# Attention and two feed-forward layers in one kernel: down products two gated blocks behind, and one rest subtracted from PSUM on VectorE

## The chip, the cores and the metric

One core of one Trainium2 chip runs the whole program. The time is the device time of one launch in microseconds; the median of three runs before the change is 899.72 us (898.28 to 900.67). Inputs and outputs are fp32.

## What is computed

The reference runs three parts in a row; the second and third take the one ahead as input. Sequence 576 and 4 batches make 2304 tokens.

```python
# attention: q, k, v of shape (4, 8, 576, 64), window of 128, a bias that falls with distance
scores = np.where(mask, scale * q @ k.T + bias, -1e9)
attn   = softmax(scores);  x = (attn @ v)            # tokens x 512
# first layer, d_ff 768
h = max(x @ w1, x @ w2, x @ w3);  y = h @ w_out      # tokens x 512
# second layer, d_ff 1536
g = y @ w_gate;  out = (g * sigmoid(g) * (y @ w_val)) @ w_out
```

## The kernel before

TensorE multiplies in the fast fp32r format, which keeps fewer bits. So every operand is held as two parts, a rounded head and the rest (operand minus head), and a product is three matmuls: head by head, head by rest, rest by head (`mm3`, L111 to L113, and L547 to L549 for the last product). `low` (L77) is the subtraction that makes a rest; `pool_round` (L80) rounds to a head on GpSimd. Weights come as 64-bit words and are turned into head and rest by `prep_w` (L90 to L99: two ScalarE and four VectorE instructions for a 128x512 tile).

The tokens are worked off in sub-chunks, (batch, half) with 256 and 320 tokens, for attention and the first layer. Attention goes in units of one head pair and one block of up to 128 queries: scores (L299, or L303 and L304), mask and softmax (L307 to L317), normalisation (L336 or L340), transposes (L349), mask selections on GpSimd (L365), values (L379 or L390), and the split of the result into head and rest. In the sub-chunks of batch 0 and the first of batch 1 the products are taken in plain fp32 (`native`), and the result comes out of PSUM in one piece: ScalarE writes the head into `x` (L384) and a copy `xr` (L385), and GpSimd subtracts the two (L77). The first sub-chunk (0, 0) has eight such units.

While the first sub-chunks are worked on, the 18 up weights of the first layer (names `w1_f_e`) are prepared; up products (`ps<-x,w`) of a sub-chunk run beside the attention of the next.

The second layer has chunks of 512 tokens (four, and a last one of 256) and 12 blocks of 128 hidden columns. `gate(c, f)` makes the two products of block f (`pg<-y,u`, 24 matmuls), then ScalarE's sigmoid (L532), two VectorE products (L533, L534), and on GpSimd the head (L80) and rest (L77) of the gated block `a`. `down(c, t, f)` multiplies block f with its output weight into PSUM (`po<-u,a`, 12 matmuls for a chunk of four tiles). The 36 weight tiles are named `u_n` with n = 3f + i: i = 0 gate, 1 value, 2 output weight. They are prepared during the end of the first layer and, three per block, in the first chunk's first blocks.

The written order sets the calls, and a list scheduler with its own timeline reorders the instructions of each engine by readiness and priority; each engine then runs its list strictly in that order. In the main loop the written order is, for block n: three weight preparations (first chunk), `gate` of block n + 1, `down` of block n. The next chunk's inputs are loaded at block `YAT`.

Of the kernel before, what the change touches and what calls it, by code (L numbers as in the profile page):

```python
# [23 lines left out]
NF1, NF2 = F1 // P, F2 // P  # L24
# [5 lines left out]
CHUNKS = [(t, min(TB, NT - t)) for t in range(0, NT, TB)]  # L30
# [3 lines left out]
C0, C1, C2, C3 = 5, 6, 12, 15  # L34
# [5 lines left out]
NORM0, K0 = "pp", 4  # L40
AH = 0, 100
A1, E1 = 3, 0
YAT = 8
LN, LT, LV = 1, 2, 4

LEAST = 1.0 * 2.0 ** -15
# [4 lines left out]
def kernel(ctx: ExitStack, tc, q0, k0, q1, k1, qk0, qk1, vv, w123, wo1, wgv, wo2, out):  # L51
# [10 lines left out]
    nc = tc.nc  # L62
# [13 lines left out]
    def low(eng, out, raw, head):  # L76
        eng.tensor_tensor(out=out, in0=raw, in1=head.bitcast(F32), op=ALU.subtract)  # L77
# [48 lines left out]
    def prep_up(f, e):  # L126
        if (f, e) not in w1:
            load_up(f, e)
        raw, w1[f, e] = w1[f, e], up_tile(f"w1_{f}_{e}")
        prep_w(raw, w1[f, e], pinned=PIN)  # L130
# [8 lines left out]
    def up_groups(b, s):  # L139

        n = SUBS[s][1]
        m = {}

        def group(f, e):
            xt = x_t[b, s]
            ps = ps_m.tile([P, 512], F32, tag="m", name="ps1")
            for k in range(KD):
                mm3(ps[:, :n], w1[f, e], k * P, xt[k][:, 0, :n], xt[k][:, 1, :n], k == 0, k == KD - 1)
            with tc.high_priority(HIGH):
                if e == 0:  # L150
                    m[f] = tmp.tile([P, 320], F32, tag="m0", name="m0")
                    nc.scalar.copy(m[f][:, :n], ps[:, :n])
                else:
                    nc.vector.tensor_tensor(out=m[f][:, :n], in0=ps[:, :n], in1=m[f][:, :n], op=ALU.max)
                if e == 2:
                    ht = hp.tile([P, 2, n], F32R, tag=f"h{s}", name=f"h{s}", bufs=NF1)
                    pool_round(ht[:, 0, :], m[f][:, :n])
                    low(nc.gpsimd, ht[:, 1, :], m[f][:, :n], ht[:, 0, :])
                    hs[b, s, f] = ht

        return [lambda f=f, e=e: group(f, e) for f in range(NF1) for e in range(3)]

    def down_groups(b, s):
        t0, n = SUBS[s]
        t0 += b * S

        def part(ps, d, ks):
            for k in ks:
                ht = hs[b, s, k]
                mm3(ps[:, :n], wo[k], d * P, ht[:, 0, :], ht[:, 1, :], k == 0, k == NF1 - 1)  # L170

        def group(ds):

            ps = [ps_m.tile([P, 512], F32, tag="m", name="ps2") for d in ds]
            for i, d in enumerate(ds):
                part(ps[i], d, range(NF1 - 1))
            for i, d in enumerate(ds):
                part(ps[i], d, [NF1 - 1])
                with tc.high_priority(HIGH):
                    y = tmp.tile([P, 2, 320], F32R, tag="y", name="y")  # L180
                    nc.scalar.copy(y[:, 0, :n], ps[i][:, :n])
                    low(nc.vector, y[:, 1, :n], ps[i][:, :n], y[:, 0, :n])
                nc.sync.dma_start(
                    out=y_dram[:, d * P:(d + 1) * P, t0:t0 + n].rearrange("a p n -> p a n"),
                    in_=y[:, :, :n].bitcast(F32),
                )

        return [lambda ds=ds: group(ds) for ds in ((0, 1), (2,), (3,))]
# [6 lines left out]
    prep = ea("prep", 4)  # L195
# [59 lines left out]
    def native(b, s):  # L255


        return b == 0 or (b, s) == (1, 0)
# [111 lines left out]
    def st_values(u):  # L370
        m = u.mq
        i0 = u.k0 // P
        v = pairs[u.b, u.s, u.p][2]
        pv = ps_v.tile([P, 2, 2, P], F32, tag="pv", name="pv")
        xr = small.tile([P, P], F32, tag="xr", name="xr")
        if native(u.b, u.s):
            for a in range(2):
                for i in range(i0, 2):
                    nc.tensor.matmul(  # L379
                        pv[a * D:a * D + D, 0, 0, :m], v[:, u.kb + i, a * D:a * D + D], u.t[:, i, 0, a, :m],  # L380
                        start=i == i0, stop=i == 1,
                    )
            xt = x_part(u)
            nc.scalar.copy(xt[:, 0], pv[:, 0, 0, :m])  # L384
            nc.scalar.copy(xr[:, :m], pv[:, 0, 0, :m])  # L385
            low(nc.gpsimd, xt[:, 1], xr[:, :m], xt[:, 0])
            return
        for a in range(2):
            for i in range(i0, 2):
                nc.tensor.matmul(  # L390
                    pv[:, a, :, :m], v[:, u.kb + i, a, :], u.t[:, i, :, a, :m], start=i == i0, stop=i == 1
                )
        c = small.tile([D, 2, P], F32, tag="c", name="c")
        nc.scalar.copy(c[:, :, :m], pv[D:P, :, 0, :m])
        nc.vector.tensor_tensor(out=c[:, :, :m], in0=pv[0:D, :, 1, :m], in1=c[:, :, :m], op=ALU.add)
        for a in range(2):
            nc.vector.tensor_tensor(
                out=xr[a * D:a * D + D, :m], in0=pv[0:D, a, 0, :m], in1=c[:, a, :m], op=ALU.add
            )
        split_x(u, xr)  # L400

    def x_part(u):
        m = u.mq
        n = SUBS[u.s][1]
        if (u.b, u.s) not in x_t:
            t = xp.tile([P, NP, 2, n], F32R, tag=f"x{u.s}", name=f"x{u.s}")
            x_t[u.b, u.s] = [t[:, p] for p in range(NP)]
        return x_t[u.b, u.s][u.p][:, :, u.q0:u.q0 + m]

    def split_x(u, xr):  # L410
        m = u.mq
        xt = x_part(u)
        pool_round(xt[:, 0], xr[:, :m])
        low(nc.gpsimd, xt[:, 1], xr[:, :m], xt[:, 0])
# [34 lines left out]
    for t in range(len(units) + LV):  # L449
        if t >= LV:  # L450
            u = units[t - LV]
            steps.append(lambda u=u: soon(st_values, u))
            if t + 1 == len(units) + LV or (units[t + 1 - LV].b, units[t + 1 - LV].s) != (u.b, u.s):
                done_at.append(len(steps))
        if 0 <= t - LT < len(units):
            steps.append(lambda u=units[t - LT]: soon(st_transpose, u))
        if 0 <= t - LN < len(units):
            steps.append(lambda u=units[t - LN]: soon(st_normalise, u))
        if t < len(units):
            u = units[t]  # L460
            if u.j == BLOCKS[u.s][0]:
                i = todo.index((u.b, u.s, u.p))
                if i == 0:
                    steps.append(begin)
                steps.append(lambda u=u, i=i: (soon(st_scores, u), prep_next(i + 1), load_next(i + 2)))
            else:
                steps.append(lambda u=u: soon(st_scores, u))
# [4 lines left out]
    def spread(main, *others, early=0):  # L472


        done = [0] * len(others)
        for i, g in enumerate(main):
            for n, o in enumerate(others):
                while done[n] < len(o) and done[n] * (len(main) - early) <= i * len(o):
                    o[done[n]]()
                    done[n] += 1  # L480
            g()
        for n, o in enumerate(others):
            for piece in o[done[n]:]:
                piece()
# [90 lines left out]
    conv = [lambda f=f, e=e: prep_up(f, e) for f in range(NF1) for e in range(3)]  # L575
# [16 lines left out]
    w2pool = en("w2pool")  # L592
    ps_o = en("ps_o", 4, space=PSUM)
    prep, load_y, gate, down = second(w2pool, raws2, ps_o)
    conv = [lambda f=f, i=i: prep(f, i) for f in range(NF2) for i in range(3)]
    spread(down_groups(*order[-2])[D6:] + up_groups(*order[-1]), [lambda: load_y(0, [0])] + conv[:C2])
    spread(down_groups(*order[-1]), [lambda: load_y(0, [1])] + conv[C2:C3])

    spread([lambda: gate(0, 0)], conv[C3:C3 + 3])
    blocks = [(c, f) for c in range(len(CHUNKS)) for f in range(NF2)]
    for n, (c, f) in enumerate(blocks):
        if c == 0:
            for piece in conv[C3 + 3 + 3 * f:C3 + 6 + 3 * f]:
                piece()
        if f == YAT and c + 1 < len(CHUNKS):
            load_y(c + 1)
        if n + 1 < len(blocks):
            gate(*blocks[n + 1])  # L610
        for t in range(CHUNKS[c][1] // P):
            down(c, t, f)

# [55 lines left out]
```

## Time and profile before

| | us |
|---|---|
| median of three runs | 899.72 |
| the profiled run's own time | 900.01 |
| its span, first to last instruction | 898.30 |
| TensorE busy | 878.1 (98%) |
| VectorE, ScalarE, GpSimd busy | 464.6, 349.5, 409.3 |
| mean granted TensorE clock | 0.996 of full |

The span is the time between the first and the last instruction of one profiled execution; the run's time has 1.7 us more around it. Busy times of TensorE are of modelled, overlapping matmuls, so start-to-start times tell more about a gap than busy time does. A wait is put down to whatever semaphore came last.

### The profile page before, as it was taken

How to read it: one execution, taken by the hardware profiler on the slowest of the kernel's cores; microseconds unless marked ns; L12 is line 12 of the kernel's file. 1: busy time of each engine (PE TensorE's matmuls, PEld its weight loads, DVE VectorE, ACT ScalarE, POOL GpSimd, SP SyncE). 2: the span in 40 equal slices, each digit the busy share in tenths (PEclk: the TensorE clock that was granted, in tenths of full speed). 3: DMA queues.
4: the chain of work that ended last, by engine and by line, in shares of the span. 5: the costliest groups of instructions: out<-in, count | busy, mean ns of one | idle time of the engine just before them, and what ended most of it. 6: DMA issues, size and time to landing. Idle time of an engine off the chain costs nothing.

```text
span 898.3 us, 14855 instructions
## 1 busy us (share of the span) xinstructions
PE 878.1 (98%) x5280; PEld 778.7 (87%) x5280; DVE 464.6 (52%) x1293; ACT 349.5 (39%) x1004; POOL 409.3 (46%) x599
## 2 busy tenths in 40 slices
PE   8998999999999999999998999999999999999998
PEld 6677899999999999999886788888888888888897
DVE  7689956867687776848999811111111111111111
ACT  6789656856486656614554301000110001000101
POOL 5587666766777586554325421222122212221222
PEclk9899999999999999999999999999999999999999
DMA  9844414415232431325755504000210002000100
GB/s 324 281 122 128 135 45 153 126 55 148 67 113 60 137 99 51 116 93 170 257 184 176 165 0 141 1 1 1 93 48 1 1 21 73 1 1 1 47 1 24
DMA packets 40873, 82.22 MB, mean 92 GB/s; under 512 B 3680, under 2 KB 16992, under 8 KB 40800
## 3 DMA queue, kind: packets, MB, share of 16 engines
q1 hardware_dynamic: 39712, 79.18, 27.5%
q10 hardware_dynamic: 1088, 2.10, 0.7%
q8 instruction: 42, 0.69, 0.3%
q14 instruction: 31, 0.25, 0.1%
HBM read 67.11 MB, written 14.16 MB: 90 GB/s over the span
## 4 chain that ended last, share of the span: by engine, by line
PE 81%; issue 6%; POOL 5%; DVE 4%; DMA 1%; ACT 1%; ACTq 0%; SPq 0%; POOLq 0%; DVEq 0%
PE ps L111 10%; PE pg L111 10%; PE pg L112 10%; PE pg L113 10%; PE ps L113 10%; PE ps L112 10%; PE po L549 5%; PE po L547 5%; PE po L548 5%; PE pv L390 2%; PE pt L349 2%; POOL a L80 1%; PE sc L299 1%; PE sc L304 1%; PE sc L303 1%
## 5 line engine op out<-in xcount | busy, mean ns | idle before, releaser
L80 POOL TENSOR_SCALAR a<-sg 128x512 fp32r<-128x512 f32 (+1 forms) x60 | 44.5, 742 | 331.8 <-DVE sg L534 328.5
L113 PE MATMUL pg<-y,u 128*128 128x512 f32 (+1 forms) x480 | 176.6, 368 | 0.0
L112 PE MATMUL pg<-y,u 128*128 128x512 f32 (+1 forms) x480 | 176.5, 368 | 0.0
L111 PE MATMUL pg<-y,u 128*128 128x512 f32 (+1 forms) x480 | 176.5, 368 | 0.0
L113 PE MATMUL ps<-x,w 128*128 128x256 f32 (+1 forms) x576 | 173.5, 302 | 1.6 <-DVE w L77 1.5
L111 PE MATMUL ps<-x,w 128*128 128x256 f32 (+1 forms) x576 | 173.3, 304 | 1.2 <-ACT w L99 1.2
L112 PE MATMUL ps<-x,w 128*128 128x256 f32 (+1 forms) x576 | 172.3, 300 | 1.9 <-POOL x L77 1.9
L533 DVE TENSOR_TENSOR sg<-pg,sg 128x512 f32<-128x512 f32 (+1 forms) x60 | 38.2, 637 | 253.8 <-ACT sg L532 253.8
L532 ACT ACTIVATE sg<-pg 128x512 f32<-128x512 f32 (+1 forms) x60 | 33.2, 553 | 325.2 <-PE pg L113 321.8
L113 PEld LDWEIGHTS ps<-x,w 128*128 128x128 f32 x576 | 109.2, 190 | 4.2 <-DVE w L77 2.4
L111 PEld LDWEIGHTS ps<-x,w 128*128 128x128 f32 x576 | 109.0, 190 | 4.0 <-ACT w L99 1.5
L112 PEld LDWEIGHTS ps<-x,w 128*128 128x128 f32 x576 | 109.2, 190 | 2.7 <-POOL x L77 2.1
L111 PEld LDWEIGHTS pg<-y,u 128*128 128x128 f32 x480 | 90.5, 188 | 15.5
L112 PEld LDWEIGHTS pg<-y,u 128*128 128x128 f32 x480 | 90.5, 188 | 15.3
L113 PEld LDWEIGHTS pg<-y,u 128*128 128x128 f32 x480 | 90.5, 188 | 15.1
L365 POOL TENSOR_SCALAR_AFFINE_SELECT t<-pk 128x512 fp32r<-128x512 f32 (+3 forms) x128 | 72.7, 590 | 34.7 <-PE pv L390 14.5
L549 PE MATMUL po<-u,a 128*128 128x512 f32 x216 | 84.2, 392 | 2.8 <-POOL a L77 2.8
L547 PE MATMUL po<-u,a 128*128 128x512 f32 x216 | 84.4, 391 | 0.3 <-POOL a L80 0.3
L548 PE MATMUL po<-u,a 128*128 128x512 f32 x216 | 84.2, 390 | 0.0
L77 POOL TENSOR_TENSOR a<-sg,a 128x512 fp32r<-128x512 f32 (+1 forms) x60 | 72.4, 1206 | 5.0
L317 ACT ACTIVATE z<-z,mn 128x128 f32<-128x128 f32 (+1 forms) x160 | 63.3, 399 | 21.8 <-DVE mn L312 21.8
L534 DVE TENSOR_TENSOR sg<-pg,sg 128x512 f32<-128x512 f32 (+1 forms) x60 | 38.2, 637 | 60.3 <-PE pg L113 60.1
(91 smaller groups left out, 1672.4 us busy)
## 6 DMA issues: line engine op xcount, KB each, us to landing
wr<-wgv SPq DMA_DIRECT2D x24, 512.0 KB, 4.2
qkr<-qk SPq DMA_DIRECT2D x24, 416.0 KB, 3.4
wr<-w SPq DMA_DIRECT2D x18, 512.0 KB, 5.2
wr<-wo SPq DMA_DIRECT2D x12, 512.0 KB, 3.9
y<-y_dram SPq DMA_DIRECT2D x12, 512.0 KB, 4.1
y_dram<-y SPq DMA_DIRECT2D x16, 320.0 KB, 2.4
out<-ob SPq DMA_DIRECT2D x18, 256.0 KB, 2.1
y_dram<-y SPq DMA_DIRECT2D x16, 256.0 KB, 2.9
```

The lines of the kernel that those rows point to most:

```text
L77: eng.tensor_tensor(out=out, in0=raw, in1=head.bitcast(F32), op=ALU.subtract)
L80: nc.gpsimd.tensor_scalar(out=out, in0=in_, scalar1=1.0, scalar2=1.0, op0=ALU.mult, op1=ALU.mult)
L111: nc.tensor.matmul(ps, wh, xt_h, start=first, stop=False)
L112: nc.tensor.matmul(ps, wh, xt_l, start=False, stop=False)
L113: nc.tensor.matmul(ps, wl, xt_h, start=False, stop=last)
L317: nc.scalar.activation(out=z[:m, a], in_=z[:m, a], func=AF.Exp, scale=-1.0, bias=mn[:m, a:a + 1], accum_out=sm[:m, a:a + 1],)
L365: nc.gpsimd.affine_select(out=t[:, i, :n, :, :m], in_=w[:, :n, :, :m], compare_op=op, fill=0.0, base=0, pattern=[[0, n], [0, 2], [-sign, m ...
L533: nc.vector.tensor_tensor(out=sg, in0=pair[0], in1=sg, op=ALU.mult)
L534: nc.vector.tensor_tensor(out=sg, in0=pair[1], in1=sg, op=ALU.mult)
L547: nc.tensor.matmul(po, ah, w2[f, 2][:, 0, :], start=f == 0, stop=False)
L548: nc.tensor.matmul(po, ah, w2[f, 2][:, 1, :], start=False, stop=False)
L549: nc.tensor.matmul(po, al, w2[f, 2][:, 0, :], start=False, stop=f == NF2 - 1)
```

## The change

There are two parts. In the second layer, `gate` of blocks 0 and 1 is issued ahead of the loop and the loop issues `gate` of block n + 2 ahead of `down` of block n; the weight preparations are put in the order of that need, and the next chunk's inputs are loaded at block 6 instead of 8. In attention, for the eight units of sub-chunk (0, 0) alone, the rest is formed by VectorE straight from PSUM, without `xr` and without GpSimd.

```diff
-YAT = 8
+YAT = 6
@@ st_values
             nc.scalar.copy(xt[:, 0], pv[:, 0, 0, :m])
+            if (u.b, u.s) == (0, 0):
+                low(nc.vector, xt[:, 1], pv[:, 0, 0, :m], xt[:, 0])
+                return
             nc.scalar.copy(xr[:, :m], pv[:, 0, 0, :m])
             low(nc.gpsimd, xt[:, 1], xr[:, :m], xt[:, 0])
@@ second layer
-    conv = [lambda f=f, i=i: prep(f, i) for f in range(NF2) for i in range(3)]
+    blocks = [(c, f) for c in range(len(CHUNKS)) for f in range(NF2)]
+    need = [(f, i) for f in range(2) for i in range(2)]
+    for f in range(NF2):
+        need += [(f + 2, i) for i in range(2) if f + 2 < NF2] + [(f, 2)]
+    conv = [lambda f=f, i=i: prep(f, i) for f, i in need]
...
-    spread([lambda: gate(0, 0)], conv[C3:C3 + 3])
+    spread([lambda: gate(0, 0), lambda: gate(0, 1)], conv[C3:C3 + 3])
...
-        if n + 1 < len(blocks):
-            gate(*blocks[n + 1])
+        if n + 2 < len(blocks):
+            gate(*blocks[n + 2])
```

On TensorE, at the down products of block 1 (output weight `u_5`) in the second layer, before; `u_7` is the value weight of block 2:

```order
L111 MATMUL pg_7156<-y_6844,u_7_6671 128x512
L112 MATMUL pg_7156<-y_6844,u_7_6671 128x512
L113 MATMUL pg_7156<-y_6844,u_7_6671 128x512
L547 MATMUL po_7097<-u_5_6605,a0_7093 128x512
L548 MATMUL po_7097<-u_5_6605,a0_7093 128x512
L549 MATMUL po_7097<-u_5_6605,a1_7094 128x512
```

The same place after the change, where `u_10` is the value weight of block 3 and lines 550 to 552 are the old 547 to 549:

```order
L111 MATMUL pg_7182<-y_6836,u_10_6704 128x512
L112 MATMUL pg_7182<-y_6836,u_10_6704 128x512
L113 MATMUL pg_7182<-y_6836,u_10_6704 128x512
L550 MATMUL po_7123<-u_5_6743,a0_7045 128x512
L551 MATMUL po_7123<-u_5_6743,a0_7045 128x512
L552 MATMUL po_7123<-u_5_6743,a1_7046 128x512
```

The gate products of block 3 now stand ahead of the down products of block 1.

On GpSimd, in the first sub-chunk (normalisations `z`, mask selections `t`, rests `x0`), before:

```order
L365 AFFINE_SELECT t_296<-pk_295 128x256 x2
L77 TENSOR_TENSOR x0_328<-xr_325,x0_328 128x128
L336 TENSOR_SCALAR z_346<-z_346,rc_371 128x128 x2
L325 TENSOR_SCALAR sm_389<-sm_389 128x2
L77 TENSOR_TENSOR x0_328<-xr_354,x0_328 128x128
L336 TENSOR_SCALAR z_387<-z_387,rc_407 128x128 x2
L365 AFFINE_SELECT t_366<-pk_365 128x256 x2
```

The same stretch of GpSimd after:

```order
L365 AFFINE_SELECT t_296<-pk_295 128x256 x2
L336 TENSOR_SCALAR z_345<-z_345,rc_369 128x128 x2
L325 TENSOR_SCALAR sm_387<-sm_387 128x2
L336 TENSOR_SCALAR z_385<-z_385,rc_404 128x128 x2
L365 AFFINE_SELECT t_364<-pk_363 128x256 x2
```

The two rests are gone from between the normalisations. On VectorE they stand among the weight preparation; the place of the first one, after:

```order
L94 SCALAR_TENSOR_TENSOR wf_237<-wr_200,wf_237 128x512
L307 COPY_PREDICATED sc_408<-later_111,fill_112 128x2x128
L331 RECIPROCAL rc_369<-sm_347 128x2
L77 TENSOR_TENSOR x0_328<-pv_324,x0_328 128x128
L96 SCALAR_TENSOR_TENSOR wr_200<-wr_200,wf_237 128x512
L93 TENSOR_SCALAR wf_306<-wf_306 128x512
```

The fourth row is new; the other five stood there before in this order.

## Rows read from the trace of the kernel before

**Rows 1.** The profile page: busy time, share of the span and instructions by engine.

```profile
PE 878.1 (98%) x5280; PEld 778.7 (87%) x5280; DVE 464.6 (52%) x1293; ACT 349.5 (39%) x1004; POOL 409.3 (46%) x599
```

**Rows 2.** Waits of TensorE: who waited for whom, us in total, times, longest.

```profile
PE po L549 <- POOL a L77: 2.8, 4, 0.9
...
PE ps L112 <- POOL x L77: 1.9, 1, 1.9
...
PE po L547 <- POOL a L80: 0.3, 1, 0.3
```

**Rows 3.** Timeline of TensorE, second layer: start, us, instruction [idle before <-releaser].

```profile
465.13 0.39 PE L547 MATMUL po<-u,a 128*128 128x512 f32 x1
...
483.54 0.39 PE L548 MATMUL po<-u,a 128*128 128x512 f32 x1
484.57 0.50 PE L549 MATMUL po<-u,a 128*128 128x512 f32 x1 [0.65 <-POOL a L77]
...
519.17 0.39 PE L547 MATMUL po<-u,a 128*128 128x512 f32 x1
...
527.33 0.39 PE L547 MATMUL po<-u,a 128*128 128x512 f32 x1
```

**Rows 4.** Stages: start:end length, busy us (count) by engine, PEclk, DMA share, GB/s.

```profile
490.00:500.00 10.00, 9.38 (x42) 7.41 (x41) 9.97 (x16) 4.20 (x8) 5.00 (x3) 1.00 0.55 175
```

**Rows 5.** Timeline of VectorE, second layer: products of two gated blocks.

```profile
485.93 0.68 DVE L533 TENSOR_TENSOR sg<-pg,sg 128x512 f32<-128x512 f32 x1
...
488.67 0.68 DVE L534 TENSOR_TENSOR sg<-pg,sg 128x512 f32<-128x512 f32 x1
...
495.05 0.68 DVE L533 TENSOR_TENSOR sg<-pg,sg 128x512 f32<-128x512 f32 x1
```

**Rows 6.** Timeline of GpSimd, second layer: with and without weight preparation on VectorE.

```profile
489.43 2.53 POOL L80 TENSOR_SCALAR a<-sg 128x512 fp32r<-128x512 f32 x1 [4.91 <-DVE sg L534]
492.05 1.59 POOL L77 TENSOR_TENSOR a<-sg,a 128x512 fp32r<-128x512 f32 x1
...
528.31 0.62 POOL L80 TENSOR_SCALAR a<-sg 128x512 fp32r<-128x512 f32 x1 [6.17 <-DVE sg L534]
529.01 1.28 POOL L77 TENSOR_TENSOR a<-sg,a 128x512 fp32r<-128x512 f32 x1
```

**Rows 7.** Stages of the first 100 us; columns PE, PEld, DVE, ACT, POOL, PEclk, DMA.

```profile
10.00:15.00 5.00, 4.36 (x29) 3.18 (x27) 4.47 (x23) 4.53 (x19) 4.15 (x12) 1.00 1.02 403
15.00:20.00 5.00, 4.07 (x28) 2.87 (x27) 4.92 (x18) 4.67 (x19) 4.84 (x8) 1.00 1.05 391
20.00:25.00 5.00, 3.72 (x25) 2.40 (x25) 4.65 (x18) 4.18 (x14) 4.75 (x10) 1.00 1.04 394
25.00:30.00 5.00, 3.76 (x18) 2.66 (x18) 3.66 (x12) 0.86 (x5) 2.79 (x6) 0.76 1.05 384
30.00:35.00 5.00, 5.00 (x22) 3.94 (x21) 1.33 (x7) 3.84 (x15) 2.41 (x5) 0.55 1.02 367
95.00:100.00 5.00, 5.00 (x38) 5.00 (x38) 5.00 (x13) 3.92 (x15) 1.96 (x3) 1.00 0.51 171
```

**Rows 8.** Timeline of VectorE, first 100 us: two idle times and the last weight rest.

```profile
31.93 0.29 DVE L312 CUSTOM_DVE_ANT_0 z<-sc,bias 128x128 f32<-128x128 f32 x1 [2.12 <-PE pt L349]
...
34.92 0.43 DVE L307 COPY_PREDICATED sc<-later,sc 128x256 f32<-128x256 int16 x1 [1.74 <-PE sc L299]
...
94.98 0.96 DVE L77 TENSOR_TENSOR w<-wr,w 128x512 fp32r<-128x512 f32 x1
```

**Rows 9.** Timeline of GpSimd: two rests of the first sub-chunk.

```profile
14.80 0.88 POOL L77 TENSOR_TENSOR x<-xr,x 128x128 fp32r<-128x128 f32 x1
...
24.54 1.64 POOL L77 TENSOR_TENSOR x<-xr,x 128x128 fp32r<-128x128 f32 x1
```

**Rows 10.** One line's instructions: ns min/median/max, first and last start us, forms.

```profile
L397 DVE TENSOR_TENSOR xr<-pv,c x104: 206/283/286, 146.2 to 404.9; 64x128 f32<-64x128 f32 x80, 64x64 f32<-64x64 f32 x24
L385 ACT COPY xr<-pv x28: 210/270/290, 13.4 to 140.2; 128x128 f32<-128x128 f32 x24, 128x64 f32<-128x64 f32 x4
```

More of the change, by code (lines that the diff above doesn't have):

```diff
@@ L594 @@
     prep, load_y, gate, down = second(w2pool, raws2, ps_o)
-    conv = [lambda f=f, i=i: prep(f, i) for f in range(NF2) for i in range(3)]
+    blocks = [(c, f) for c in range(len(CHUNKS)) for f in range(NF2)]
[3 more added lines that the diff above has]
+    conv = [lambda f=f, i=i: prep(f, i) for f, i in need]
     spread(down_groups(*order[-2])[D6:] + up_groups(*order[-1]), [lambda: load_y(0, [0])] + conv[:C2])
     spread(down_groups(*order[-1]), [lambda: load_y(0, [1])] + conv[C2:C3])
-    spread([lambda: gate(0, 0)], conv[C3:C3 + 3])
-    blocks = [(c, f) for c in range(len(CHUNKS)) for f in range(NF2)]
+    spread([lambda: gate(0, 0), lambda: gate(0, 1)], conv[C3:C3 + 3])
     for n, (c, f) in enumerate(blocks):
```

## Prediction

> **What bounds the kernel now.** The share of busy time comes first: TensorE 98%, every other engine about half [rows 1]. So the time is TensorE's work plus what TensorE loses, and the change removes none of its products: 5,280 stay 5,280. The question is only where it loses time. The list of TensorE's waits names the two places that the change touches: the down products (L547, L549) wait for GpSimd's halves of the gated block, and an up product (L112) waits 1.9 us for GpSimd's rest of the attention result [rows 2]. Both lists are short because a modelled matmul end hides part of each gap, so I measure the loss by start times instead.
>
> In the second layer, the down products of blocks 1, 7 and 8 start at 465.13, 519.17 and 527.33 us [rows 3]. Without preparation beside them, blocks lie 8.16 us apart (7 to 8). From 1 to 7 six blocks took 54.04 us, where 6 x 8.16 = 48.96: TensorE loses 5.1 us there. Inside such a block the third product, L549, starts 1.03 us after the one ahead of it and is put down to GpSimd [rows 3]. The pace is VectorE's: it is busy 9.97 of 10 us [rows 4], and its first product of a gated block comes at 485.93 and again at 495.05, 9.12 us later [rows 5]. With that VectorE load GpSimd's rounding takes 2.53 us and its subtraction 1.59; once VectorE is free, 0.62 and 1.28 [rows 6]. The gated block is late for two reasons, VectorE's queue and GpSimd's long instructions, and the down products follow only one block behind.
>
> In the first 100 us the load is on the other engines. From 10 to 25 us VectorE, ScalarE and GpSimd are each over 80% busy and TensorE waits between them; from 25 to 35 us there is a hole: VectorE does 3.66 + 1.33 us of work in 10, and the granted clock falls to 0.76 and 0.55 in those stretches [rows 7]. From 95 us TensorE is full [rows 7], one block after the last rest of an up weight is made at 94.98 [rows 8]. So what delays VectorE's weight preparation before 95 us delays everything behind it, and what TensorE saves there stays saved.
>
> **Part one: down products two blocks behind.** It adds no instruction. Each gated block gets 8.16 us more (one gate product group and one down group) before it is wanted. VectorE does 9.12 us of work for a block where TensorE needs 8.16 [rows 3, 5], so TensorE gains 0.96 us on it per block, over the six blocks in which weights are prepared at most 5.8 us. The added 8.16 us cover that with 2.4 us to spare, and the stall does not come back as another: the PSUM buffers of a gate group are needed again two groups later in both orders, and the two scratch tiles of the gate are freed by GpSimd's subtraction, which then ends some 5 us after VectorE's second product [rows 5, 6]. So I take the whole 5.1 us. The lower bound is what the list of waits shows, 2.8 + 0.3 = 3.1 us [rows 2]. The new preparation order (gate and value weights of two blocks first, the output weight of a block when its down products are near) is the same 36 weights on the same VectorE; it is hidden by the distance of the preparation, whose last rest is needed only in the last blocks. Without that cover a missing weight would cost 2.5 to 3 us, a third of the 9.12. The later chunks' inputs are loaded at block 6 instead of 8, since their gate now comes a block earlier; nothing is queued behind those loads on SP's queue but output stores of a chunk's end. Cost nothing; a late load would show as a TensorE wait at a chunk's start. The end of the kernel keeps its last three product groups: nothing.
>
> **Part two: the first sub-chunk's rest on VectorE.** Removed: eight copies on ScalarE of 0.27 us [rows 10] and eight GpSimd subtractions. The two in the rows took 0.88 and 1.64 us [rows 9], and TensorE's 1.9 us wait ends with the second. The order also shows GpSimd's mask selections move up behind the normalisations. Added: eight VectorE subtractions of 128x128 from PSUM. No row shows that form; the nearest is L397 (PSUM and SBUF into SBUF, 128 columns), 0.283 us [rows 10], so 8 x 0.28 = 2.2 us. Below nothing it cannot be. VectorE is 89 to 98% busy from 10 to 25 us [rows 7], so the five or so that fall there cost their full time, 1.4 us; those in the hole are hidden. Each also waits for ScalarE's head, and behind it in VectorE's queue stand the weight preparation and the next scores.
>
> The gain has two ends. At least the 1.9 us wait of TensorE goes [rows 2]. At most the whole hole of VectorE goes: 10 - 3.66 - 1.33 = 5.0 us [rows 7], since its two long idle times, 2.12 and 1.74 us, end with TensorE's transposes and scores [rows 8], which stood behind the blocked product. I take the middle, 3.4 us, since the removed wait is directly ahead of the hole but not its only cause. Net: -3.4 + 1.4 = -2.0 us, with ends of -1.9 + 2.2 = +0.3 and -5.0 + 1.4 = -3.6.
>
> The rest of the schedule moves too: four attention units fewer stand ahead of the last up weight on VectorE. That is 8 softmax inputs, 3 mask copies and 3 key rests, some 5 us by L312's and L307's rows at 0.29 and 0.43 us [rows 8] and about 0.6 us for a key rest (an estimate). But TensorE loses about as much work of its own to later, so I count nothing, with an end of -2.7. Against it, the last attention result of the second sub-chunk is ready later; a late one costs at most a GpSimd subtraction, 1.6 us [rows 9].
>
> A GpSimd subtraction of one size takes 0.88 or 1.64 us here, and the rounding 2.53 or 0.62 [rows 6, 9]: beside a busy VectorE it stretches. The Trainium skill (SBUF — State Buffer, Who interferes with whom) says that a VectorE instruction with at most one SBUF input, outside the two-port modes, does not contend with GpSimd; the new subtraction reads one operand from PSUM, so by that rule it adds nothing to GpSimd's time. If it stretched GpSimd as the rows show for other work, part two's gain would shrink by up to 0.8 us each. No row of this form can show which.
>
> **Sum.** The profiled run took 900.01 us (span 898.30, 1.71 around it), 0.29 above the median of 899.72. 900.0 - 5.1 - 2.0 = 892.9, against the median 892.6.
>
> **The rivals.**
> - The hole closes and the clock stays up. For it: GpSimd has no spare time ahead of the hole. Against: VectorE and ScalarE are nearly as full, so TensorE stays as idle as it was. The Trainium skill (TensorE: Matmul & The Clock Gate, Part 1) says that the throttled state is the default and activity releases it; the two low clock rows behind the thinly used stretch agree. Price: -3.6 and the clock of 30 to 35 us, 5 x 0.45 = 2.25 us [rows 7]. 900.0 - 5.1 - 3.6 - 2.2 = 889.1, or 888.8.
> - Part two brings nothing, because VectorE's pace to 95 us swallows it: 900.0 - 5.1 = 894.9, or 894.6.
> - Part two costs: VectorE waits at two of the rests for about 2 us each [rows 8]: 898.9, or 898.6.
> - Part one does not do what it says: the late VectorE products keep TensorE at 9.12 us per block through scratch or PSUM buffers: 900.0 - 2.0 = 898.0, or 897.7.
> - Slower: VectorE's queue blocks at the rests. Five of the eight stand where the attention chain is slow; each waits 1.93 us, the mean of 2.12 and 1.74 [rows 8], with the weight preparation behind it: 9.7 + 2.2 = 11.9 us, 906.5. It decides from 7.8 us on (5.1 and the 2.7 us of the bound below). Against it: VectorE has 5 us of idle time there already.
>
> **How the numbers follow.** About 0.3%, 2.7 us, is what a measurement of this kernel can tell from no change: faster means under 897.0, slower over 902.4. Forecast 892.6 with its own range of 890 to 894.5: 0.45. Hole and clock: 0.17. Part two nothing: 0.17. Part two costs: 0.07. Part one without effect: 0.07. Slower: 0.07. Faster 0.79, same 0.14, slower 0.07. The range leaves out the slower case and half of each end: 888 to 898.
>
> **What would show it.** Part one: down products 8.1 to 8.2 us apart from the second block on, no wait of L547 or L549 for GpSimd, and GpSimd's 2.5 us roundings still there. Part two: L112's wait for the result gone, VectorE's idle times in 25 to 35 us shorter, the last up weight ready 1 to 4 us before 94.98. The prediction is wrong if the second layer shows new waits on the gate's own products, if VectorE sits idle ahead of the PSUM subtractions, or if the middle of the kernel, which I left out (100 to 435 us), moves by more than 1 us.

## The result, and the profile after

The changed kernel takes 891.6 us (median of four runs, 888.6 to 892.0) where the kernel before took 899.5 beside it: a ratio of 0.9906, 95% interval 0.9884 to 0.9927. Measured again in another group it was 891.1 and 0.9906 (0.9878 to 0.9935). The forecast was 892.6. The profiled execution took 892.0 us with a span of 890.30.

The page's busy times, and the first rows of TensorE's waits (who waited for whom, us in total, times, longest), to be held against [rows 1, 2]:

```profile
PE 875.6 (98%) x5280; PEld 777.8 (87%) x5280; DVE 467.8 (53%) x1301; ACT 347.8 (39%) x996; POOL 401.1 (45%) x591
```

```profile
PE sc L299 <- DVE mn L312: 2.2, 5, 0.6
PE pt L349 <- ACT z L340: 1.3, 1, 1.3
...
PE pg L111 <- DVE y L77: 0.8, 1, 0.8
```

The down products are gone from the list, and so is the up product that waited 1.9 us for the attention result. VectorE has eight instructions more, ScalarE and GpSimd eight less each. The two longest of the new waits are shown: transposes wait for ScalarE's `z`, and a gate product for `y`.

Timeline of TensorE in the second layer, lines 550 to 552 being the old 547 to 549 [rows 3]: the layer's first gate product and the gap behind it, the starts of blocks 1, 5, 7 and 8, and the one gap left between blocks.

```profile
441.61 0.39 PE L111 MATMUL pg<-y,u 128*128 128x512 f32 x1
...
446.85 0.39 PE L113 MATMUL pg<-y,u 128*128 128x512 f32 x1
448.05 0.50 PE L111 MATMUL pg<-y,u 128*128 128x512 f32 x1 [0.81 <-DVE y L77]
...
467.22 0.39 PE L550 MATMUL po<-u,a 128*128 128x512 f32 x1
...
499.86 0.39 PE L550 MATMUL po<-u,a 128*128 128x512 f32 x1
500.09 0.39 PE L551 MATMUL po<-u,a 128*128 128x512 f32 x1
500.62 0.50 PE L552 MATMUL po<-u,a 128*128 128x512 f32 x1
...
516.63 0.39 PE L550 MATMUL po<-u,a 128*128 128x512 f32 x1
...
524.79 0.39 PE L550 MATMUL po<-u,a 128*128 128x512 f32 x1
```

Blocks 1 to 7 now take 49.41 us instead of 54.04; each lies 8.16 behind the one ahead but block 6, at 8.61. VectorE is as full as before in 490 to 500 us (9.97 of 10 [rows 4]), but TensorE notices it only ahead of block 6.

The first 100 us, where [rows 7] had the hole from 25 to 35 us (columns PE, PEld, DVE, ACT, POOL, PEclk, DMA share, GB/s):

```profile
25.00:30.00 5.00, 4.14 (x26) 2.96 (x25) 4.42 (x15) 4.38 (x15) 2.56 (x4) 1.00 1.05 383
30.00:35.00 5.00, 4.92 (x33) 3.02 (x32) 4.62 (x21) 4.28 (x15) 2.32 (x4) 1.00 1.06 378
70.00:75.00 5.00, 3.07 (x12) 1.75 (x13) 3.75 (x16) 4.16 (x16) 2.05 (x6) 0.70 0.00 0
75.00:80.00 5.00, 5.00 (x34) 4.88 (x32) 4.37 (x12) 0.85 (x6) 3.29 (x7) 0.62 0.27 82
```

VectorE's idle time in 25 to 35 us fell from 5.0 to 1.0 us and the granted clock is full there. But another hole opens at 70 us, and the granted clock is at its lower level (1.2 of 2.4 GHz) from 72.0 to 78.8, about as long as before from 27.6 to 34.5. These rows show how it opens (GpSimd, VectorE, ScalarE, TensorE):

```profile
65.42 3.34 POOL L365 TENSOR_SCALAR_AFFINE_SELECT t<-pk 128x128 f32<-128x128 f32 x2
...
70.93 0.22 DVE L331 RECIPROCAL rc<-sm 64x2 f32<-64x2 f32 x2 [2.25 <-POOL sm L325]
...
71.13 1.28 ACT L340 ACTIVATE z<-z,rc 64x128 f32<-64x128 f32 x4 [0.84 <-DVE rc L331]
...
71.58 0.58 PE L349 MATMUL pt<-ident,z 64*128 64x64 f32 x2 [1.31 <-ACT z L340]
```

Two GpSimd mask selections take 3.34 us together beside a nearly full VectorE (3.29 us of work in the 3.40 from 65.4 us on). The tiny sum behind them in GpSimd's queue, with four other instructions between (L325, adding 1e-9 to the softmax's denominator), comes late, VectorE's reciprocal waits 2.25 us for it at the head of its queue, and TensorE's transposes 1.31 us behind that.

**Where the time went**, by the start of the same product in the two profiled executions. From block 1 on the changed kernel has one gate group (24 of the 36 products of a block, 5.44 us) more behind it, which is taken off here. Each of the two executions holds one stretch at the lower clock of some 7 us in the first 100 us. The first gate product before:

```profile
446.06 0.39 PE L111 MATMUL pg<-y,u 128*128 128x512 f32 x1
```

| | before | after | difference |
|---|---|---|---|
| first gate product of the second layer | 446.06 | 441.61 | -4.45 |
| down products of block 1 | 465.13 | 461.78 | -3.35 |
| down products of block 7 | 519.17 | 511.19 | -7.98 |
| span | 898.30 | 890.30 | -8.00 |

So attention and first layer gave 4.45 us, the start of the second layer took 1.1 back (0.97 of it in the gap at 446.85), its blocks gave 4.63, and the rest is equal: from block 7 to the end both take 379.1 us. The earlier load of the next chunk's inputs, which was not run alone, changes nothing there that can be seen.

### The profile page after: what moved, and what is told of

It reads as the page before. It is cut to its first block, busy times and chain, and to the rows that moved or that the text cites. A ratio compares the mean times of both kernels' runs of the same rounds, so it can differ in the third digit from the quotient of the medians.

```text
span 890.3 us, 14848 instructions
## 1 busy us (share of the span) xinstructions
PE 875.6 (98%) x5280; PEld 777.8 (87%) x5280; DVE 467.8 (53%) x1301; ACT 347.8 (39%) x996; POOL 401.1 (45%) x591
## 4 chain that ended last, share of the span: by engine, by line
PE 83%; issue 6%; POOL 4%; DVE 3%; DMA 1%; ACT 1%; ACTq 0%; SPq 0%; POOLq 0%; DVEq 0%
PE ps L113 10%; PE ps L111 10%; PE ps L112 10%; PE pg L113 9%; PE pg L111 9%; PE pg L112 9%; PE po L552 5%; PE po L550 5%; PE po L551 5%; PE pv L393 2%; PE sc L299 2%; PE pt L349 2%; POOL a L80 1%; PE pv L379 1%; PE sc L304 1%
## 5 line engine op out<-in xcount | busy, mean ns | idle before, releaser
L112 PE MATMUL pg<-y,u 128*128 128x512 f32 (+1 forms) x480 | 176.6, 368 | 0.0
L111 PE MATMUL ps<-x,w 128*128 128x320 f32 (+1 forms) x576 | 172.4, 303 | 1.1 <-ACT m L152 0.8
L113 PE MATMUL ps<-x,w 128*128 128x320 f32 (+1 forms) x576 | 173.2, 302 | 0.1
L112 PE MATMUL ps<-x,w 128*128 128x320 f32 (+1 forms) x576 | 172.6, 300 | 0.0
L112 PEld LDWEIGHTS ps<-x,w 128*128 128x128 f32 x576 | 109.5, 190 | 1.2 <-issue 0.9
L112 PEld LDWEIGHTS pg<-y,u 128*128 128x128 f32 x480 | 90.5, 188 | 15.5
L365 POOL TENSOR_SCALAR_AFFINE_SELECT t<-pk 128x512 fp32r<-128x512 f32 (+3 forms) x128 | 81.0, 655 | 46.2 <-PE pv L393 20.5
```

The source lines that it names most:

```text
L111: nc.tensor.matmul(ps, wh, xt_h, start=first, stop=False)
L112: nc.tensor.matmul(ps, wh, xt_l, start=False, stop=False)
L113: nc.tensor.matmul(ps, wl, xt_h, start=False, stop=last)
L365: nc.gpsimd.affine_select(out=t[:, i, :n, :, :m], in_=w[:, :n, :, :m], compare_op=op, fill=0.0, base=0, pattern=[[0, n], [0, 2], [-sign, m ...
```

## The experiments

Ratios are against runs of the kernel before on the same chip, with 95% intervals.

**Each part alone.** First part two alone:

```diff
             nc.scalar.copy(xt[:, 0], pv[:, 0, 0, :m])
+            if (u.b, u.s) == (0, 0):
+                low(nc.vector, xt[:, 1], pv[:, 0, 0, :m], xt[:, 0])
+                return
```

> Only part two: the first sub-chunk's rest from PSUM on VectorE; the second layer as before. Theory (the parts add; part two fills the hole of VectorE at 25 to 35 us): the products of the middle of the kernel start 4 us earlier than before and the second layer still loses 5 us, so about 895.5 us, ratio 0.9956. Rival (the early shift is lost again without part one, since VectorE's weight preparation for the second layer is the next bound): 899 us, ratio 1.0.

Measured: 897.71 us, ratio 0.9984 (0.9971 to 0.9996), between the two expectations. Then part one alone, the same lines out of the changed kernel:

```diff
-            if (u.b, u.s) == (0, 0):
-                low(nc.vector, xt[:, 1], pv[:, 0, 0, :m], xt[:, 0])
-                return
```

> Only part one: down products two blocks behind, with the new preparation order and the earlier load; attention as before. Theory: down products 8.1 to 8.2 us apart from block 1 on, 4 to 5 us gained, about 895 us, ratio 0.995. Rival (part one's gain needs the earlier start of the second layer): under 2 us, ratio 0.998 or more.

Measured: 892.55 us, ratio 0.9940 (0.9919 to 0.9960). Blocks 1 to 7 take 48.96 us, six times 8.16 to the last digit: the 5.1 us of the stall are gone whole. The time fell by more, 5.4 us by the ratio and 6.5 by the medians, but the clocks differ: these four executions had a mean granted clock of 0.998 to 1.000, those of the kernel before beside them 0.995 to 1.000. Among executions at 0.999 or 1.000 the medians are 892.54 (three) and 897.75 (five), 5.2 us apart.

Part two alone is worth 1.4 us; beside part one 3.1 by the ratios (0.9940 less 0.9906, both with intervals of some 2 us to either side) and 1.0 by the medians. These two intervals overlap, so the times by themselves do not show what part two adds to part one. The traces do. Up to the second layer TensorE's order is one and the same in the kernel before and in part one alone, and another one in the changed kernel and in part two alone. The first gate product starts at 446.06 and 443.73 us in the first two, at 441.61 and 440.21 in the other two, and of these four executions only that of part one alone had no stretch at the lower clock ahead of it. So in attention and first layer part two gives some 2 us at least, as far as single executions tell.

The trace of part two alone shows why it is worth less alone. The first gate product comes 5.85 us earlier than before, but one block behind the second layer gives 2.3 us of it back (blocks 1 to 7 take 56.34 us against 54.04, some 1.7 of it in a stretch at the lower clock around 492 us that opens behind these waits). TensorE's list of waits:

```profile
PE po L552 <- POOL a L77: 2.5, 3, 0.9
...
PE po L550 <- POOL a L80: 1.8, 2, 1.6
```

The longest of these waits, 1.6 us, ends with a rounding on GpSimd that took 4.67 us, where [rows 6] have 2.53:

```profile
483.83 4.67 POOL L80 TENSOR_SCALAR a<-sg 128x512 fp32r<-128x512 f32 x1 [4.92 <-DVE sg L537]
```

VectorE makes the rests of these blocks' weights 1.8 to 4.9 us earlier than before, so late weights are not the reason. Two blocks behind, a rounding of that length costs the changed kernel 0.45 us (below).

**The order of preparation.**

```diff
-    conv = [lambda f=f, i=i: prep(f, i) for f, i in need]
+    conv = [lambda f=f, i=i: prep(f, i) for f in range(NF2) for i in range(3)]
```

(on part one alone)

> Part one alone, with the weights of the second layer prepared in the old order (gate, value, output weight of a block, block by block). If the new order is only neutral, as the prediction had it: the same as part one alone with the new order, ratio 0.993 to 0.996. If the old order makes a gate or value weight late (each is wanted a block earlier than before, and an output weight stands ahead of them): one to three waits of the gate's products for weights of 1 to 3 us, ratio 0.996 to 1.0.

Measured: 892.84 us, ratio 0.9932 (0.9913 to 0.9951), blocks 1 to 7 in 48.96 us, no wait for a weight in the second layer. TensorE's order is the same with both, and the new order of preparation is neutral as far as these runs can tell.

**Whose pace was it?** In the kernel before, GpSimd's rounding of the gated block goes to ScalarE; one block behind as it was.

```diff
-                pool_round(ah, sg)
+                nc.scalar.copy(ah, sg)
```

> The kernel before, one block behind as it was, with the head of the gated block rounded by a ScalarE copy instead of GpSimd's 2.5 us rounding (L80). Theory A (GpSimd's stretched rounding and subtraction are what makes the gated block late): blocks 1 to 7 of the second layer come 8.2 to 8.5 us apart instead of 9.0, the time is 3 to 4.5 us less, ratio 0.995 to 0.997. Theory B (VectorE's queue, 9.1 us of work per block, sets the pace, as the prediction said): the blocks stay 8.8 to 9.1 us apart and the ratio is 0.999 to 1.001.

Measured: 895.23 us, ratio 0.9961 (0.9951 to 0.9971): the time of theory A, but the blocks lie 8.71 us apart, between the two theories, as the starts of blocks 3 and 4 on TensorE's timeline show. The window over them has VectorE (the third busy figure) at 9.96 of 10:

```profile
479.44 0.39 PE L547 MATMUL po<-u,a 128*128 128x512 f32 x1
...
488.15 0.39 PE L547 MATMUL po<-u,a 128*128 128x512 f32 x1
```

```profile
480.00:490.00 10.00, 9.49 (x41) 7.52 (x41) 9.96 (x16) 5.88 (x10) 2.28 (x2) 1.00 0.57 193
```

VectorE still sets the pace, but its work for a block is not a fixed 9.12 us. In the kernel before, GpSimd's subtraction lies on two of VectorE's instructions; first GpSimd's row, then VectorE's, with the same two lines ahead of it, where GpSimd's rounding lies on them and leaves them at 0.68:

```profile
482.93 1.59 POOL L77 TENSOR_TENSOR a<-sg,a 128x512 fp32r<-128x512 f32 x1
```

```profile
480.14 0.68 DVE L94 SCALAR_TENSOR_TENSOR wf<-wr,wf 128x512 int32<-128x512 int32 x1
480.74 0.68 DVE L77 TENSOR_TENSOR u<-wr,u 128x512 fp32r<-128x512 f32 x1
...
482.39 0.99 DVE L94 SCALAR_TENSOR_TENSOR wf<-wr,wf 128x512 int32<-128x512 int32 x1
483.30 1.76 DVE L77 TENSOR_TENSOR u<-wr,u 128x512 fp32r<-128x512 f32 x1
```

They cost VectorE 0.31 + 1.08 = 1.39 us more. With the rounding on ScalarE the subtraction falls on one instruction:

```profile
478.23 2.02 POOL L77 TENSOR_TENSOR a<-sg,a 128x512 fp32r<-128x512 f32 x1 [6.69 <-ACT a L537]
```

```profile
479.14 1.66 DVE L94 SCALAR_TENSOR_TENSOR wf<-wr,wf 128x512 int32<-128x512 int32 x1
```

That is 0.98 more. The difference, 0.41, is the difference of the paces, 9.12 - 8.71 = 0.41. Over blocks 1 to 7 it gives 2.4 us (51.65 against 54.04); the time gained 3.5 by the ratio and 3.8 by the medians, and the 1.1 to 1.4 us beyond it stay open. The clock is not all of it: among executions at one mean clock, 1.000 or 0.998, the medians still differ by 3.4 and 3.5.

**What part two takes away.** Three loads could make the difference: ScalarE's copy, GpSimd's subtraction, and the longer way to the rest. Each kernel below is the changed one with something put back; where the rest still comes straight from PSUM, what the added instructions make is not used.

```diff
-                low(nc.vector, xt[:, 1], pv[:, 0, 0, :m], xt[:, 0])
+                nc.scalar.copy(xr[:, :m], pv[:, 0, 0, :m])
+                low(nc.vector, xt[:, 1], xr[:, :m], xt[:, 0])
```

> The change, but in the first sub-chunk ScalarE still copies the result into xr and VectorE subtracts from that copy. It puts back the eight ScalarE copies (8 x 0.27 us) and leaves GpSimd relieved. Theory (GpSimd's relief makes part two's gain): within 1.5 us of the change, 891 to 893 us, ratio 0.991 to 0.993. Rival (the copy on a full ScalarE and the longer way to the rest were the cost): 894 to 896 us, ratio 0.994 to 0.996.

Measured: 894.56 us, ratio 0.9957 (0.9943 to 0.9971). That is the time of the rival, by which the copy and the longer way to the rest were the cost; the order changed too, and the kernels below put the copy back without the longer way.

```diff
                 low(nc.vector, xt[:, 1], pv[:, 0, 0, :m], xt[:, 0])
+                nc.scalar.copy(xr[:, :m], pv[:, 0, 0, :m])
+                low(nc.gpsimd, xr[:, :m], xr[:, :m], xt[:, 0])
```

> The change, but ScalarE still makes the copy and GpSimd still makes its subtraction, in place and read by nobody, while VectorE makes the rest that is used. So the path is the new one and the old load on ScalarE and GpSimd is back. Theory (GpSimd's load ahead of the normalisations and mask selections is what is saved): most of part two's 4 us is lost, 894.5 to 896 us, ratio 0.9945 to 0.996. Rival (what counts is that TensorE no longer waits for GpSimd's place in the queue): 891 to 893 us, ratio 0.991 to 0.993.

Measured: 892.19 us, ratio 0.9934 (0.9911 to 0.9957): between the changed kernel and part one alone, so it could not decide. The two loads were therefore put back one at a time, GpSimd's first:

```diff
                 low(nc.vector, xt[:, 1], pv[:, 0, 0, :m], xt[:, 0])
+                low(nc.gpsimd, xr[:, :m], xt[:, 0].bitcast(F32), xt[:, 0])
```

> The changed kernel, with one more GpSimd subtraction of 128x128 in each of the eight units, head minus head into an unused tile: GpSimd has the number of instructions that it had before, ScalarE's second copy stays out. With copy and subtraction both added back the time was 892.2, no better than part one alone. If GpSimd's load is what part two takes away: 892 to 894. If it is ScalarE's copy: 888.6 to 892, like the changed kernel. If neither but the order that the scheduler makes of it: no relation to the load, anything from 888 to 896, and the added copy by itself as free to fall anywhere.

Measured: 888.95 us (888.32 to 889.89), ratio 0.9877 (0.9856 to 0.9898).

```diff
                 low(nc.vector, xt[:, 1], pv[:, 0, 0, :m], xt[:, 0])
+                nc.scalar.copy(xr[:, :m], pv[:, 0, 0, :m])
```

> The changed kernel, with ScalarE's second copy of the result out of PSUM added back in each of the eight units, into an unused tile; no GpSimd subtraction. If ScalarE's 0.27 us per unit (or the longer hold of the PSUM buffer) is what part two takes away: 892 to 894. If it is GpSimd's load: 888.6 to 892. If it is the order: anything from 888 to 896.

Measured: 891.08 us (889.84 to 892.51), ratio 0.9900 (0.9877 to 0.9923). The changed kernel beside them took 891.13 (below). GpSimd's load put back makes nothing slower: its four runs have a median 2.2 us lower. ScalarE's copy put back changes nothing that intervals of 2 us to either side can tell. By what was expected of them, the first points at ScalarE's copy and the second at GpSimd's load, so no account by one load alone fits both.

What changes beside the loads is the order. The first 570 TensorE products of the kernel before (all that start before 100 us) and of part one alone stand in exactly the same order; between before and after only two thirds match (buffer numbers left out, matched in sequence), between the changed kernel and these two variants about 70%, the one with the copy on the way half.

One pair has the load changed and the order not. The kernel with both put back and the one with the copy alone have the same order on TensorE, VectorE and ScalarE through the whole program, and GpSimd has the eight subtractions more. Here the load does cost: 1.1 us by the medians, 3.1 by the ratios, though the intervals overlap (0.9911 to 0.9957 against 0.9877 to 0.9923). The traces agree. Two products of TensorE, first with the copy alone, then with both, from ahead of the added subtractions and from behind six of the eight (the longer time of the second row is the lower clock, from 40.8 us on in that execution):

```profile
13.80 1.10 PE L299 MATMUL sc<-kn,qz 128*128 128x256 f32 x4 [0.42 <-DVE mn L312]
...
40.94 1.13 PE L379 MATMUL pv<-t,vn 128*64 128x128 f32 x8 [1.16 <-ACT xr L387]
```

```profile
15.30 1.10 PE L299 MATMUL sc<-kn,qz 128*128 128x256 f32 x4 [0.34 <-DVE mn L312]
...
43.38 0.66 PE L379 MATMUL pv<-t,vn 128*64 128x128 f32 x8 [1.15 <-ACT xr L387]
```

The second execution starts late by 1.50 us and is 2.44 behind at the second product: 0.94 us more. So with the order held, GpSimd's load costs about a microsecond in these executions, and the order that comes with a load can outweigh it, as the subtraction alone shows.

**More of the same.** VectorE forms the rest in both sub-chunks of batch 0:

```diff
-            if (u.b, u.s) == (0, 0):
+            if u.b == 0:
```

> The changed kernel, with VectorE forming the rest from PSUM in both sub-chunks of batch 0, twenty units instead of eight. If the gain of part two comes from the load taken off GpSimd: another 1 to 3 us, 888.5 to 890.5, and the last up weight earlier again. If it comes from the one spot where TensorE stood behind a late rest, and VectorE is the fuller engine to 95 us: 12 x 0.28 = 3.4 us more on VectorE, no gain or up to 3 us lost, 891.5 to 894.5.

Measured: 894.78 us (891.47 to 896.91), ratio 0.9951 (0.9934 to 0.9968): slower than the changed kernel by about what twelve more VectorE instructions of 0.28 us come to. That is the second expectation: not more gain from less GpSimd, although the order changes here too.

**The hop of the softmax sum.** The hole at 70 us began with a sum that came back late from GpSimd. On the changed kernel:

```diff
-        if native(u.b, u.s):
-            nc.gpsimd.tensor_scalar(
-                out=u.sm[:m], in0=u.sm[:m], scalar1=1e-9, scalar2=1.0, op0=ALU.add, op1=ALU.mult
-            )
-        else:
-            nc.vector.tensor_scalar(out=u.sm[:m], in0=u.sm[:m], scalar1=1e-9, scalar2=None, op0=ALU.add)
+        nc.vector.tensor_scalar(out=u.sm[:m], in0=u.sm[:m], scalar1=1e-9, scalar2=None, op0=ALU.add)
```

> The changed kernel, with the 1e-9 added to the softmax sum (L325) on VectorE also in the plain fp32 sub-chunks, where GpSimd did it. In the changed kernel a GpSimd mask selection of 3.34 us at 65.42 us made this sum late; VectorE's reciprocal then waited 2.25 us, the transposes 1.31 us behind it, and the granted clock fell to its lower level from 72.0 to 78.8 us. Theory (the hop to GpSimd and back opens that hole): the wait of the reciprocal goes, no half clock lies between 70 and 80 us, and the time is 1 to 4 us under the changed kernel, 888 to 890.5. Rival (the hole has no single cause, another one opens elsewhere in the first 100 us): 891 to 893.

Measured: 887.21 us (886.71 to 891.83), ratio 0.9885 (0.9858 to 0.9913), the fastest kernel of the study by its median, 4 us under the changed kernel by the medians and 1.9 by the ratios. The intervals overlap, but three of its four executions, 886.7 to 887.4, lie under all eight of the changed kernel. Its windows, for comparison with those of the changed kernel, show no hole and full clock in both places:

```profile
25.00:30.00 5.00, 4.65 (x32) 3.62 (x30) 5.00 (x18) 4.13 (x14) 2.32 (x3) 1.00 1.03 372
...
70.00:75.00 5.00, 5.00 (x43) 3.97 (x41) 5.00 (x20) 4.02 (x19) 1.27 (x4) 1.00 0.31 105
75.00:80.00 5.00, 3.88 (x32) 2.99 (x30) 5.00 (x14) 4.39 (x14) 4.02 (x6) 1.00 0.24 65
```

That looks like a proof of the cause. The same edit on part one alone, without part two:

> Part one, and the softmax sum (L325) on VectorE in the plain fp32 sub-chunks, but without part two: the result's rest again by copy and GpSimd. If the hop of the sum through GpSimd costs time by itself: 888.5 to 890.5, 2 to 4 us under part one alone (892.55). If it only costs something once VectorE waits less elsewhere (that is, after part two): 892 to 893.

Measured: 899.28 us, ratio 0.9994 (0.9979 to 1.0009); both expectations missed. The edit costs 6.7 us there by the medians (4.9 by the ratios), and all that part one had gained, though the second layer is as in part one alone (48.96 us). Its longest wait and two windows:

```profile
PE ps L113 <- DVE w L77: 5.5, 4, 2.9
```

```profile
85.00:90.00 5.00, 1.97 (x13) 1.35 (x11) 5.00 (x10) 3.48 (x13) 2.33 (x3) 0.88 0.33 95
90.00:95.00 5.00, 4.39 (x20) 4.39 (x21) 5.00 (x19) 4.39 (x12) 1.29 (x2) 0.50 0.49 160
```

TensorE is busy 1.97 of 5 us in the first, and the granted clock is at its lower level behind it: up products were placed ahead of weights that a full VectorE had not made yet, and they block TensorE's queue for 5.5 us. Before, these waits for weights came to 1.5 us. The edit is the same, the order that the scheduler makes of it is not, and the two results lie on opposite sides.

**The changed kernel again**, nothing edited:

> The changed kernel once more, beside the others of this group on the same chip, for its executions at full clock and those with a half clock stretch. Expected 888.3 to 889 at a mean granted clock of 1.000, and 891 to 892 where one stretch of some 7 us at half clock falls into it (3.4 us more): both kinds should show, and their difference is the stretch's price. If the difference is not the clock's, times at 1.000 spread over the whole 888 to 892.

Measured: 891.13 us (889.83 to 894.60), ratio 0.9906. The expectation missed: no execution had a mean clock of 1.000, one at 0.996 took 890.58 and one 891.68. The slowest, 894.60, is the profiled one, with a longer gap at the second layer's start than the 0.97 us of the other execution (first fence, TensorE's timeline) and two stretches at the lower clock (second, windows):

```profile
449.48 0.50 PE L111 MATMUL pg<-y,u 128*128 128x512 f32 x1 [2.56 <-DVE y L77]
```

```profile
75.00:80.00 5.00, 5.00 (x35) 4.88 (x35) 4.89 (x17) 1.92 (x12) 3.54 (x7) 0.66 0.27 82
...
450.00:455.00 5.00, 5.00 (x16) 3.95 (x16) 4.18 (x9) 3.83 (x7) 0.58 (x1) 0.66 0.60 188
```

The wait for `y` comes over ScalarE's split, which waits for the store of an earlier `y`, 1.81 us in this execution:

```profile
448.47 0.43 ACT L181 CAST y<-ps 128x320 fp32r<-128x320 f32 x1 [1.81 <-DMA y_dram<-y]
```

So the executions of one kernel differ by more than the clock in the attention: the wait for `y` took 0.8 or 2.6 us, and the clock fell behind the longer one.

## Why the prediction was right

**Part one, 5.1 us: right, by its own steps.** Alone it takes exactly the 5.1 us that the block starts gave, not the 3.1 of the list of waits, and the time agrees at like clocks (5.2). VectorE's pace was the bound, as said, and the experiment with the rounding on ScalarE refined it: 1.4 of VectorE's 9.12 us are GpSimd's subtraction lying on its instructions. The new order cost nothing, and the list of waits shows no late load at a chunk's start. Inside the changed kernel 4.63 us came, since the spare time was shorter than the 2.4 us reckoned: one rounding took 4.68 us, not 2.5, the rest of gated block 5 came late, and block 6 lies 0.45 us further behind:

```profile
494.20 4.68 POOL L80 TENSOR_SCALAR a<-sg 128x512 fp32r<-128x512 f32 x1 [4.92 <-DVE sg L537]
498.95 1.61 POOL L77 TENSOR_TENSOR a<-sg,a 128x512 fp32r<-128x512 f32 x1
```

In the second profiled execution a rounding of 4.68 us too cost nothing (blocks 1 to 7 in 48.96 us); there TensorE had come later, behind the longer wait for `y`.

**What it left out at the layer's start.** The prediction named new waits on the gate's own products as a sign against it. One came, but not through buffers: TensorE, earlier by 4.45 us, met `y` (0.81 us), and 1.1 us went back there, 4.5 in the second profiled execution. Of its three signs of being wrong two showed, this one and the middle of the kernel (below); the third did not, since VectorE sat idle ahead of none of the eight PSUM subtractions.

**Part two, 2.0 us: the size is not contradicted, the working did not hold.** The cost of the added instruction was right, 0.28 forecast, though three of the eight start before 25 us and not five:

```profile
L77 DVE TENSOR_TENSOR x<-pv,x x8: 268/276/284, 14.5 to 41.1; 128x128 fp32r<-128x128 f32 x8
```

L112's wait went, and most of VectorE's hole with it. Measured beside part one, part two is worth 1.0 us by the medians and 3.1 by the ratios, alone 1.4; the forecast lies among them, and the runs do not fix the size better than that. Three steps failed.

- The last up weight was ready 9.7 us earlier, not 1 to 4: the last rest of an up weight starts at 85.32 instead of 94.98 [rows 8] (92.25 in part one alone, whose clock stayed up).

```profile
85.32 0.68 DVE L77 TENSOR_TENSOR w<-wr,w 128x512 fp32r<-128x512 f32 x1
```

  More than half of that went back, since products of the next units, which stood ahead of the last up product before, now stand behind it: from some 110 us to 390 us the same products come some 3.5 to 4.4 us earlier. The sentence that TensorE loses about as much work of its own to later had the sign and the kind of it, not the size. In the three kernels with copy, subtraction or both put back beside the direct rest the last weight comes at 82.9 to 85.7 us, so this head start does not tell their times apart; with the copy on the way it comes at 88.8.
- The gain was worked out as a load taken off GpSimd plus a hole half closed. Half of that hole was the clock's and not the blocked product's: in part one alone, with the same order, the same 1.90 us wait and the clock up, VectorE is idle for 2.5 us in 25 to 35 us and not 5.0 (2.5 too in the two other kernels of that order), and the idle time of 2.12 us that the prediction put behind the blocked product [rows 8] is 0.34:

```profile
30.41 0.29 DVE L312 CUSTOM_DVE_ANT_0 z<-sc,bias 128x128 f32<-128x128 f32 x1 [0.34 <-PE pt L349]
```

  So the upper end of 5.0, and with it the middle of 3.4, was too high. And putting the load back cost about 1 us in one order and nothing in another. The term was a sum over instructions where the result is a new order; the softmax sum on VectorE, 1.9 to 4 us to the good in one order and 4.9 to 6.7 to the bad in the other, shows how far such a sum can be off for edits of this size.
- The middle of the kernel moved by more than 1 us, as the first point says. At a product near 412 us the lead is down to 2.7 (a new 0.96 us gap at 405.21), and at 446 it is 4.45 again, since a stall of 1.6 us at 435 us is gone.

**The rivals.** "The hole closes and the clock stays up" came half true: the hole closed, the clock was up in 25 to 35 us, and a new hole with the lower clock came at 72. One execution of the first measurement at a mean clock of 1.000 took 888.62, which is that rival's 888.8. "Part two brings nothing" and "part two costs", 894.6 and 898.6, lie above seven of the eight executions (the eighth took 894.60), and part two alone is faster than the kernel before, if by little (0.9971 to 0.9996). "Part one without effect" is refuted by part one alone, "the queue blocks at the rests" by VectorE's 4.42 and 4.62 us of work in the two stretches of the old hole.

**What stays open** is which feature of the order in the first 100 us makes part two's gain. The loads were put back one at a time and both together, but the order held still between only two of these kernels, and never between one of them and the changed kernel, so load and order are separated for GpSimd's subtraction alone, in an order that is not the changed kernel's. The sum of the profile's rows does not give the gain. It was luck in part that the total held: that 892.6 came within 1.0 us of the measured 891.6 owes something to errors that cancelled: by the profiled executions part one with the layer's start gave 3.5 us instead of 5.1, attention and first layer 4.45 instead of 2.0.

## What to carry to other kernels

Measure a stall by the starts of the products and not by the list of waits, and ask which engine sets the pace: one block more of distance hides a producer that falls behind for a limited number of blocks. Where a scheduler makes the order, a small edit in a stretch in which all engines are full can change that order, and the order's effect was larger here than the edit's own (from 2 to 4 us gained to 5 to 7 lost for the same edit); its instruction costs bound little, so measure it next to an edit that does nothing, look for pairs of kernels in which the order stayed, and compare executions at the same granted clock. And test a good edit again on another base before its cause is believed.

## What the runs showed of the hardware

- **GpSimd and VectorE stretch each other.** GpSimd's rounding took 0.62 us alone, 0.99 to 4.68 beside weight preparation; VectorE's instructions beside it stayed at 0.68. Beside GpSimd's subtraction of two SBUF operands, VectorE's instructions of 0.68 us took up to 1.76. The eight subtractions that read PSUM stayed at 0.268 to 0.284 us although five of them overlap a GpSimd instruction. The Trainium skill (SBUF — State Buffer, Who interferes with whom) has the two engines contend for one shared pair of ports as an exclusive lock, with a VectorE instruction of at most one SBUF input, outside the two-port modes, free of it; these rows agree on VectorE's side. Whether GpSimd's instructions beside them were stretched, no run here shows.
- **The clock differs between executions of one order.** Part one alone has the order of the kernel before in the first 100 us and the same wait of TensorE ahead of the hole (1.90 us), and its profiled execution kept the full clock there:

```profile
25.00:30.00 5.00, 3.50 (x23) 2.63 (x23) 3.86 (x12) 1.58 (x9) 3.06 (x6) 1.00 1.03 372
30.00:35.00 5.00, 5.00 (x36) 3.75 (x35) 3.67 (x16) 5.00 (x20) 3.81 (x6) 1.00 1.05 367
```

  [rows 7] have 0.76 and 0.55 there, and the products behind it come 2.73 us later; one of them, first in the kernel before, then in part one alone:

```profile
36.02 1.03 PE L299 MATMUL sc<-kn,qz 128*64 128x256 f32 x4
```

```profile
33.29 1.03 PE L299 MATMUL sc<-kn,qz 128*64 128x256 f32 x4
```

  Over the 47 executions of the kernel before beside the experiments, 14 at a mean clock of 1.000 have a median of 897.7 us, 17 at 0.995 or 0.996 one of 900.6. A comparison of two profiled executions can be off by that much, and the 4.45 us of attention and first layer above hold one such stretch on both sides.
